# A gated linear-attention layer feeding a two-layer network on one core: first-chunk sums and state decays moved onto TensorE, one PSUM pool, and a new order of steps

## The chip, the core and the metric

The kernel runs on one core of a Trainium2 chip. Its time is the device time of one execution in microseconds (us). Five instruction streams work side by side: TensorE (PE, with its weight loads, PEld), VectorE (DVE), ScalarE (ACT), GpSimd (POOL) and SyncE (SP), which here issues every DMA. Each stream takes its instructions strictly in the order in which the program wrote them, and waits where an operand, a buffer or a PSUM bank is not ready.

## What is computed

For 4 batches and 8 heads (32 sequences of 768 steps, head size 40) the reference runs an mLSTM cell, and then a feed-forward network on all 3072 tokens (320 to 2048 to 320):

```python
for t in range(S):                                   # S = 768
    m_new  = np.maximum(f_gate[:, :, t] + m, i_gate[:, :, t])
    f_stab = np.exp(f_gate[:, :, t] + m - m_new)
    i_stab = np.exp(i_gate[:, :, t] - m_new);  m = m_new
    C = f_stab * C + i_stab * np.einsum('bhd,bhe->bhde', vt, kt)
    n = f_stab * n + i_stab * kt
    h_tilde = np.einsum('bhde,bhe->bhd', C, qt)
    denom = np.maximum(np.abs(np.einsum('bhd,bhd->bh', n, qt)[:, :, None]), 1.0)
    y[:, :, t] = sigmoid(o_gate[:, :, t]) * h_tilde / denom
h = y_as_tokens @ w_in                               # 3072 x 320 @ 320 x 2048
g = np.where(h >= 1, h, np.where(h <= -1, 0.0, (h + 1) ** 2 / 4))
out = g @ w_out                                      # 2048 x 320
```

## The kernel before

**Tiles.** The 768 steps are cut into 6 chunks of 128. A tile n is one chunk of one batch (chunk n // 4, batch n % 4; 24 tiles, eight heads each). A tile has these steps: `load_qk`, `load_v`, `load_A` (loads); `score` (16 products of keys and queries into two PSUM banks, then two VectorE products with the decay matrix A, one for each half of four heads); `main` (16 products of the masked scores with the gated values; from chunk 1 on also products with the carried state; then the denominator z, the gated output y, three transposes, a cast and two subtractions, which put the tile's y as a pair of words xh, xl into the network's input X[j]); `carry` (from chunk 0 on: six products keys by values, a mask, the decay of the old state by `dec`, an addition).

**Decay matrices.** In chunk 0 (tiles 0 to 3) the matrix is built on TensorE: `exponents` (steps E) writes a causal mask of -30000 into two PSUM banks, `add_sums` (A) adds the running gate sum of the column step by products with a one-hot matrix `pick`, and `decay` (x) takes eight exponentials of 128x128, each with the row step's sum `nA` as its bias. `first_sums` (p) makes that `nA` for chunk 0. In chunks 1 to 4 the sums go through a DRAM tensor `a_d` and come back broadcast (`load_A`), POOL masks them, ACT takes the exponentials. The gates of chunks 1 to 4 are worked out in one batch: `batch_maxima` (b), `batch_sums` (g1), `batch_tail` (tail.1), `batch_exps` (exps.1). `batch_exps` also makes the decay of the state for each sequence and chunk, writes it to DRAM (`dc_d`) in 40 copies and reads it back in 12 DMAs of 4-byte elements into `dec`, which lies by head dimension. `decays` does the same for one chunk.

**Network.** 512 tokens (four tiles) are a block j. For each of 16 slices fc of the 2048 columns `mm1` makes 8 products (the weights as pairs of words wh, wl), `relu` two ACT passes, `largest` (max) one VectorE pass, and `mm2` (out) adds into four PSUM banks that stay open for the whole block. Before block 0 the weights come as packed words: `load_w` (W.k) loads one of 16 pieces of 768 or 640 KB into one of three buffers `wraw`, and `convert` (w.k, seven steps for a piece of w_in, five for one of w_out) turns it into fp32 on ACT and VectorE. The fourth step is the last that reads the piece's buffer.

**Order.** The string STEPS lists, one after the other, every step of chunk 0, of chunk 1 and of block 0, with loads and conversions in between; each engine's queue is that list cut down to its own instructions. The mark `--` ends the front: the pool `gate` is closed and the network's buffers take its place. After STEPS the blocks 1 to 5 run in a loop with attention tiles 8 to 23 laid in by a plan. A step `w9`, `w2` or `w1` in the front asks for that many products of a zero matrix ahead of the next PSUM tile (`hot`); by STEPS there are 32 of them. PSUM is cut into three pools: two banks for attention (`psa`), two for mm1 (`psh`), four for mm2 (`pso`); only in the front does `psum_a` deal all eight out in turn.

Of the kernel before, what the change touches and what calls it, by code (L numbers as in the profile page):

```python
# [111 lines left out]
def mlstm_ffn_kernel(ctx, tc, qk, qn, vk, og, fi0, fi, fib, w_in, w_out, cst, out):  # L112
# [23 lines left out]
    ident = const.tile([P, P], F32, name="ident")  # L136
# [66 lines left out]
    def batch_maxima():  # L203
# [798 lines left out]
```

## Time and profile before

| | |
|---|---|
| median of 3 runs | 504.64 us (503.70 to 505.88) |
| the profiled execution | 506.14 us, of which 504.4 us from its first to its last instruction |
| PE busy | 488.2 us (97%) |
| DVE, ACT, POOL busy | 338.5, 303.0, 112.8 us |
| mean granted TensorE clock | 0.983 |

The profile gives each engine's busy time, the clock that TensorE was granted, and for an instruction the idle time of its engine before it and what ended that. A busy PE is a PE with a product in flight: at the lower clock the same product stays longer, so a busy PE may also be a slow one.

### The profile page before, as it was taken

How to read it: one execution, taken by the hardware profiler on the slowest of the kernel's cores; microseconds unless marked ns; L12 is line 12 of the kernel's file. 1: busy time of each engine (PE TensorE's matmuls, PEld its weight loads, DVE VectorE, ACT ScalarE, POOL GpSimd, SP SyncE). 2: the span in 40 equal slices, each digit the busy share in tenths (PEclk: the TensorE clock that was granted, in tenths of full speed). 3: DMA queues.
4: the chain of work that ended last, by engine and by line, in shares of the span. 5: the costliest groups of instructions: out<-in, count | busy, mean ns of one | idle time of the engine just before them, and what ended most of it. 6: DMA issues, size and time to landing. Idle time of an engine off the chain costs nothing.

```text
span 504.4 us, 8805 instructions
## 1 busy us (share of the span) xinstructions
PE 488.2 (97%) x3396; PEld 419.2 (83%) x3399; DVE 338.5 (67%) x621; ACT 303.0 (60%) x576; POOL 112.8 (22%) x120
## 2 busy tenths in 40 slices
PE   8799979999999999999999989999999999999996
PEld 4687757877788899888899878889888889989996
DVE  5689767978778986668875668757666745544332
ACT  6548958768587446596355596444587544365553
POOL 3020421150422423122422235312321200000000
PEclk9959997999999999999999999999999999999999
DMA  8975585550631132231322332222431000010001
GB/s 231 291 248 180 148 268 195 214 187 3 192 116 60 68 110 91 71 114 57 104 43 84 120 123 109 68 79 63 157 104 58 16 1 1 0 54 0 1 2 52
DMA packets 29646, 51.48 MB, mean 102 GB/s; under 512 B 10060, under 2 KB 19940, under 8 KB 29604
## 3 DMA queue, kind: packets, MB, share of 16 engines
q1 hardware_dynamic: 29604, 50.92, 31.6%
q8 instruction: 27, 0.44, 0.4%
q14 instruction: 15, 0.12, 0.1%
HBM read 46.80 MB, written 4.04 MB: 101 GB/s over the span
## 4 chain that ended last, share of the span: by engine, by line
PE 74%; ACT 4%; DVE 1%; issue 0%; ACTq 0%
PE pso L98 31%; PE psh L98 30%; PE psa L98 13%; ACT Abc L98 1%; ACT L98 1%; ACT r L98 1%; ACT sig L98 1%; DVE y L98 0%; ACT gh L98 0%; DVE gl L98 0%; DVE r L98 0%; DVE sz L98 0%; DVE z L98 0%; ACTq L997 0%; DVE v L98 0%
## 5 line engine op out<-in xcount | busy, mean ns | idle before, releaser
L98 ACT ACTIVATE r<-psh,half 128x512 f32<-128x512 f32 x96 | 65.7, 685 | 95.1 <-PE psh L98 94.9
L98 DVE SCALAR_TENSOR_TENSOR r<-psh,r 128x512 f32<-128x512 f32 x96 | 66.0, 688 | 62.8 <-ACT r L98 62.4
L98 PE MATMUL pso<-oh,gh 128*128 128x320 f32 x320 | 100.8, 317 | 1.8 <-ACT gh L98 1.6
L98 PE MATMUL psh<-xh,wh 128*128 128x512 f32 x288 | 101.5, 406 | 0.0
L98 PE MATMUL psh<-xh,wl 128*128 128x512 f32 x288 | 99.8, 398 | 0.4 <-DVE wl L98 0.4
L98 PE MATMUL pso<-ow,gh 128*128 128x320 f32 x320 | 99.4, 312 | 0.0
L98 PE MATMUL pso<-oh,gl 128*128 128x320 f32 x320 | 95.6, 312 | 0.0
L98 DVE TENSOR_TENSOR gl<-r,gh 128x512 fp32r<-128x512 f32 x80 | 63.1, 789 | 40.7 <-ACT gh L98 40.5
L98 ACT CAST gh<-r 128x512 fp32r<-128x512 f32 x80 | 49.4, 618 | 54.2 <-DVE r L98 53.6
L98 PEld LDWEIGHTS pso<-oh,gh 128*128 128x128 f32 x320 | 60.1, 188 | 6.9 <-ACT gh L98 1.8
L98 PEld LDWEIGHTS psh<-xh,wl 128*128 128x128 f32 x288 | 54.5, 190 | 13.2 <-DVE wl L98 0.8
L98 PEld LDWEIGHTS pso<-ow,gh 128*128 128x128 f32 x320 | 60.2, 188 | 3.0
L98 ACT ACTIVATE r<-r 128x512 f32<-128x512 f32 x96 | 60.7, 632 | 2.7
L98 PE MATMUL psh<-xl,wh 128*128 128x512 f32 x192 | 62.0, 401 | 0.0
L98 PEld LDWEIGHTS pso<-oh,gl 128*128 128x128 f32 x320 | 59.3, 188 | 0.3
L98 PEld LDWEIGHTS psh<-xh,wh 128*128 128x128 f32 x288 | 50.5, 190 | 6.5 <-DVE r L98 0.2
L98 ACT ACTIVATE Abc<-Abc,nA 128x128 f32<-128x128 f32 x160 | 50.2, 391 | 0.8 <-POOL Abc L98 0.7
L98 POOL TENSOR_TENSOR v<-vk,G 128x328 f32<-128x328 f32 x36 | 30.4, 851 | 63.5 <-issue 42.5
L98 PEld LDWEIGHTS psh<-xl,wh 128*128 128x128 f32 x192 | 36.2, 190 | 8.4
L98 POOL TENSOR_SCALAR_AFFINE_SELECT Abc<-Abc 128x1024 f32<-128x1024 f32 x20 | 24.5, 1226 | 80.2 <-DMA Abc<-a_d 60.9
L98 PE MATMUL pso<-ow,r 128*128 128x320 f32 x128 | 37.7, 440 | 0.0
L98 POOL TENSOR_TENSOR m<-m 128x1024 bf16<-128x1024 f32 x12 | 23.4, 1949 | 50.6 <-DVE m L98 50.6
(174 smaller groups left out, 674.8 us busy)
## 6 DMA issues: line engine op xcount, KB each, us to landing
Abc<-a_d SPq DMA_DIRECT2D x20, 512.0 KB
raw<-in_qk SPq DMA_DIRECT2D x48, 160.0 KB
vk<-in_vk SPq DMA_DIRECT2D x20, 324.0 KB
wraw<-in_w_in SPq DMA_DIRECT2D x8, 768.0 KB
wraw<-in_w_out SPq DMA_DIRECT2D x8, 640.0 KB
sig<-in_og SPq DMA_DIRECT2D x6, 640.0 KB
out<-r SPq DMA_DIRECT2D x24, 160.0 KB
qn<-in_qn SPq DMA_DIRECT2D x20, 180.0 KB
```

Of the source, the lines that this page charges most:

```text
L98: r = getattr(self.engine, name)(*args, **kwargs)
```

## The change

It does seven things. (1) `first_sums` and `nA` for chunk 0 go; `add_sums` ends in a product with `less` (minus `pick`) in each half, which subtracts the row's sum in PSUM, and `decay` takes one exponential of 128x512 for each half. (2) `dc_d`, `dc`, `decays` and the 15 reads into `dec` go; `batch_decays` (decs) takes one exponential of a 128x16 one-hot matrix with the decay as its bias, three small products and one copy; `heads` (one) builds the left factor once on POOL. (3) All eight PSUM banks are one pool `ps`. (4) The zero products are asked for by steps of their own, `hot.k`, ten in all. (5) `batch_maxima`, `batch_sums` and `batch_tail` are cut into 2, 3 and 4 steps that can be placed apart. (6) The constants `head_of` and `own` come with `ident`. (7) STEPS is a new list, from the first load to the end of block 0. The mm, relu, max, out, W, w and attention steps of tiles 4 to 9 in it are the same in number.

```diff
-    ps_a = ctx.enter_context(tc.tile_pool(name="ps_a", bufs=2, space=PSUM))
-    ps_h = ctx.enter_context(tc.tile_pool(name="ps_h", bufs=2, space=PSUM))
-    ps_o = ctx.enter_context(tc.tile_pool(name="ps_o", bufs=4, space=PSUM))
+    ps = ctx.enter_context(tc.tile_pool(name="ps", bufs=8, space=PSUM))
...
+    less = gate.tile([3 * NSEQ, NSEQ], BF16, name="less")
+    nc.vector.tensor_scalar(out=less, in0=pick, scalar1=-1.0, scalar2=None, op0=ALU.mult)
...
-        dx = mid.tile([P, D], F32, name="dx_b")
-        nc.scalar.activation(dx, mb["dc"].broadcast_to([P, D]), AF.Exp)
-        nc.sync.dma_start(dc_d[1:5].rearrange("c b (h d) -> (c b h) d", d=D), dx)
+    def heads():
+        T["one"] = mb["all"][:, 1, :DM]
+        nc.gpsimd.tensor_copy(T["one"].rearrange("p (h d) -> p h d", d=D), head_of.unsqueeze(2).broadcast_to([P, H, D]))
+
+    def batch_decays(n):
+        e = mb["all"][:, 1, DM:DM + B * B]
+        nc.scalar.activation(e, own, AF.Exp, bias=mb["dc"])
+        dp = psum_a()[:120, :3 * B * B]
         for g, h0 in enumerate(GROUPS):
-            for c in range(1, 5):
-                nc.sync.dma_start(dec[:, g, :, c], dc_d[c, :, h0 * D:(h0 + 3) * D].rearrange("b x -> x b"))
+            nc.tensor.matmul(dp[:, g * B * B:(g + 1) * B * B],
+                             T["one"][:, h0 * D:(h0 + 3) * D], e, start=True, stop=True)
+        yield
+        nc.scalar.copy(dec[:, :, :, 1:5], dp.rearrange("p (g b c) -> p g b c", g=3, b=B))
...
                 nc.tensor.matmul(ps[hh][:, h * L:(h + 1) * L], pick[:, k:k + 1].broadcast_to([3 * NSEQ, P]),
-                                 top(T["ac"]), start=False, stop=h == 3)
+                                 top(T["ac"]), start=False, stop=False)
+            k = b * H + 4 * hh
+            nc.tensor.matmul(ps[hh], top(T["ac"]), less[:, k:k + 4].unsqueeze(2).broadcast_to([3 * NSEQ, 4, L]),
+                             start=False, stop=True)
...
+        if c == 0:
+            nc.scalar.activation(A[:, 4 * hh:4 * hh + 4, :], T[n]["Ap"][hh].rearrange("p (h t) -> p h t", t=L), AF.Exp)
+            return
...
-        hp = ps_h.tile([P, 512], F32, name="psh")[:, :TT]
+        hp = psum_a()[:, :TT]
```

The head of STEPS, up to the first steps of block 0, before and after (numbers behind a dot are tiles, pieces or halves; `fi`, `fb`, `qk`, `vv`, `v`, `og`, `id`, `cs`, `W`, `A` are loads; `mask` is the old E, `add` the old A, `dec` the old x, `gex` the old h):

```diff
-    "Lg Li Lo Lq0 Lv0 Lq1 Lw0 Lf Lq2 Lv2 Lq3 Lw1 Lc o w9 E0 g0 p A0 k0 x00 w2 s0 W.6 x01 m00 w1 E1 v.6 A1 h0 v0 "
-    "x10 m01 W.2 w2 s1 x11 v1 m10 c w2 u0 v.0 m11 b w2 E2 w.1 A2 x20 w2 s2 y0 w.1 x21 v2 w.1 m20 m21 w2 u1 w.1 z0 "
-    "w2 E3 A3 x30 e v2.0 w2 s3 v3 w.1 y1 x31 t0 m30 m31 w2 u2 z1 y2 w2 v.1 u3 v.3 t1 z2 qk.4 v2.1 w.2 W.3 y3 w2 "
-    "v.2 t2 z3 qk.5 w.2 og.1 v2.3 w.2 W.4 t3 d g1 -- A.4 v2.2 carry.0 carry.3 A.5 mm.0 mm.1 w.2 relu.0 w.2 carry.3 "
+    "fi.0 sums.0 mask.3 W.0 w.0 mask.1 gtail.0 mask.0 vv.0 w.0 qk.0 fb.0 mask.2 w.0 add.0 bmax.0 dec.0.0 qk.1 "
+    "add.1 w.0 id.0 add.3 dec.1.1 qk.2 add.2 score.0 w.0 dec.0.1 dec.2.0 dec.2.1 vv.2 gex.0 bmax.0 score.0 v1.1 "
+    "one.0 hot.2 score.1 score.0 og.0 v1.0 dec.1.0 score.2 score.1 score.1 score.2 v1.3 main.0 v1.2 score.2 main.1 "
+    "qk.3 W.1 v.0 bsum.0 v.4 dec.3.0 v.1 bsum.0 main.2 bsum.0 v.5 sig.0 btail.0 main.0 btail.0 btail.0 main.1 "
+    "score.3 dec.3.1 w.1 btail.0 main.0 main.0 hot.4 main.0 W.2 main.2 main.1 v2.0 exps.0 score.3 w.0 main.1 cs.0 "
+    "score.3 main.0 main.2 main.3 main.1 v2.4 carry.0 main.2 hot.2 main.1 main.3 decs.0 main.2 w.1 w.1 carry.4 "
+    "hot.2 w.1 main.3 main.3 main.2 main.3 W.3 w.2 A.5 v2.1 v2.5 A.4 w.0 W.4 w.2 w.1 main.3 carry.0 prep.5 carry.1 "
+    "qk.4 carry.5 W.5 -- w.2 w.2 w.2 qk.5 carry.1 mm.0 mm.1 relu.0 W.6 w.2 main.4 relu.1 w.3 carry.4 W.7 w.2 w.3 "
+    "max.0 main.5 mm.3 relu.3 w.3 decs.0 prep.4 v.6 mm.2 max.1 w.3 A.6 max.3 relu.2 v.2 main.5 carry.4 w.4 main.4 "
+    "w.4 w.3 max.2 v1.4 out.0 carry.5 prep.5 carry.5 w.4 w.4 A.7 prep.4 v1.5 qk.6 w.5 out.1 ..."
```

## Rows read from the trace of the kernel before

**Rows 1.** The page: its first line, the busy line, and the granted TensorE clock in 40 equal slices of the span (9 is 90% or more).

```profile
span 504.4 us, 8805 instructions
...
PE 488.2 (97%) x3396; PEld 419.2 (83%) x3399; DVE 338.5 (67%) x621; ACT 303.0 (60%) x576; POOL 112.8 (22%) x120
...
PEclk9959997999999999999999999999999999999999
```

**Rows 2.** Busy time by stage: the stretch, its length, busy time of PE, PEld, DVE, ACT and POOL (with instructions), then granted clock, DMA share and GB/s.

```profile
12.30:26.70 14.40, 11.82 (x104) 9.03 (x104) 9.60 (x18) 8.14 (x22) 1.17 (x2) 1.00 0.95 287
26.70:38.26 11.56, 11.35 (x57) 9.96 (x57) 9.62 (x27) 3.72 (x9) 3.56 (x5) 0.56 0.75 249
38.26:72.88 34.62, 33.70 (x187) 25.64 (x185) 26.29 (x54) 26.29 (x47) 8.26 (x8) 1.00 0.63 179
72.88:75.84 2.96, 0.00 (x0) 0.03 (x1) 2.75 (x5) 2.93 (x7) 0.00 (x0) 0.83 1.02 408
75.84:82.50 6.66, 6.66 (x21) 5.44 (x22) 5.55 (x10) 5.48 (x9) 1.09 (x1) 0.56 0.83 276
...
104.00:400.00 296.00, 293.54 (x2219) 256.30 (x2219) 215.96 (x381) 181.35 (x351) 86.65 (x81) 1.00 0.29 93
```

**Rows 3.** The timeline of the front, the first uses of three loads: start, duration, engine, operation; in brackets the engine's idle time before it and what ended it.

```profile
2.83 0.48 DVE L98 TENSOR_TENSOR_SCAN m<-fi,m 96x128 f32<-96x128 f32 x1 [1.91 <-DMA fi<-in_fi]
...
13.70 0.89 ACT L98 ACTIVATE mg<-wraw 128x768 f32<-128x768 f32 x1 [0.47 <-DMA wraw<-in_w_in]
...
17.47 0.74 POOL L98 TENSOR_TENSOR ow<-ow,G 128x328 f32<-128x328 f32 x1 [4.73 <-DMA ow<-in_vk]
```

**Rows 4.** The timeline of PE: tile 0's 16 products in `main`, tile 2's transposes, two zero products, tile 3's 16 products, two carries' 12 products, the first mm1, and one carry's six products in block 0.

```profile
12.86 1.88 PE L98 MATMUL psh<-ow,Abc 128*128 128x41 f32 x16
...
29.40 0.88 PE L98 MATMUL pso<-ident,y 128*128 128x128 f32 x3
30.07 1.06 PE L98 MATMUL psa<-zeros 128*128 128x512 bf16 x2
30.92 3.48 PE L98 MATMUL psa<-ow,A 128*128 128x41 f32 x16
...
36.84 1.67 PE L98 MATMUL psa<-ow 128*120 128x123 f32 x12
38.26 0.70 PE L98 MATMUL psh<-xh,wh 128*128 128x512 f32 x2
...
57.69 0.87 PE L98 MATMUL psa<-v,vk 128*120 128x123 f32 x6 [0.20 <-issue]
```

**Rows 5.** VectorE: groups by shape from 0 to 38.3 us (busy us and mean ns, then idle before them), and its busy time in the two stretches that hold the batch sums and the batch tail.

```profile
L98 DVE TENSOR_TENSOR Abc<-pso,Abc 128x512 f32<-128x512 f32 x4 | 2.8, 692 | 3.6 <-ACT Abc L98 3.6
...
L98 DVE TENSOR_TENSOR_SCAN m_r<-fi_r,m_r 32x512 f32<-32x512 f32 x1 | 1.8, 1821 | 0.0
...
L98 DVE TENSOR_TENSOR y<-psa,sz 128x320 f32<-128x320 f32 x2 | 1.0, 491 | 0.1
L98 DVE SCALAR_TENSOR_TENSOR win<-mg,win 128x768 int32<-128x768 int32 x1 | 1.0, 958 | 0.1
L98 DVE TENSOR_TENSOR xl<-psa,xh 128x256 fp32r<-128x256 f32 x2 | 0.8, 414 | 0.0
...
L98 DVE RECIPROCAL z<-z 128x8 f32<-128x8 f32 x4 | 0.8, 203 | 0.1
...
39.20:41.00 1.80, 1.66 (x8) 1.00 0.00 0
43.60:45.70 2.10, 1.96 (x9) 1.00 0.81 321
```

**Rows 6.** SyncE's queue: when a DMA instruction started and how long it held the queue.

```profile
19.35 5.34 SPq L98 DMA_DIRECT2D m_b<-m_r  x4
...
51.01 0.33 SPq L98 DMA_DIRECT2D dc_d<-dx_b  x1
56.64 7.05 SPq L98 DMA_DIRECT2D dec<-dc_d  x12
...
64.81 0.35 SPq L98 DMA_DIRECT2D wraw<-in_w_out  x1
```

**Rows 7.** The timeline around PE's longest wait.

```profile
72.02 0.77 ACT L98 ACTIVATE mg<-wraw 128x640 f32<-128x640 f32 x1 [5.33 <-DMA wraw<-in_w_out]
...
72.83 0.49 DVE L98 TENSOR_SCALAR mg<-mg 128x640 f32<-128x640 f32 x1 [3.27 <-ACT mg L98]
...
75.06 0.68 DVE L98 TENSOR_TENSOR Abc<-psa,Abc 128x512 f32<-128x512 f32 x1
...
75.84 1.55 PE L98 MATMUL psa<-v,vk 128*120 128x123 f32 x6 [2.96 <-issue]
```

**Rows 8.** ACT's groups by shape from 38 to 104 us, columns as in Rows 5.

```profile
L98 ACT ACTIVATE Abc<-Abc,nA 128x128 f32<-128x128 f32 x43 | 13.5, 389 | 0.7 <-POOL Abc L98 0.7
L98 ACT ACTIVATE r<-psh,half 128x512 f32<-128x512 f32 x10 | 6.7, 674 | 3.6 <-PE psh L98 3.6
...
L98 ACT ACT_TABLE_LOAD x2 | 2.6, 1283 | 0.0
...
L98 ACT CAST xh<-psa 128x384 fp32r<-128x384 f32 x2 | 0.9, 462 | 0.0
...
L98 ACT ACTIVATE dx_b<-dc_b 128x40 f32<-128x40 f32 x1 | 0.2, 248 | 0.0
```

More of the change, by code (lines that the diff above doesn't have):

```diff
@@ L134, in mlstm_ffn_kernel @@
     nc.gpsimd.memset(zeros, 0.0)
-    ident = const.tile([P, P], F32, name="ident")
+    id_t = const.tile([P, P + H + B * B], F32, name="ident")
+    ident = id_t[:, :P]
+    head_of = id_t[:, P:P + H]
+    own = id_t[:, P + H:]
     cs_t = const.tile([120, 9 * D1], F32, name="cs")
@@ L157, in mlstm_ffn_kernel @@
     nA = const.tile([P, NC, NSEQ], F32, name="nA")
-    dc = const.tile([NSEQ, NC], F32, name="dc")
-    dc_d = dr.tile([NC, B, H * D], F32, name="dc_d")
     dec = const.tile([120, 3, B, NC], F32, name="dec")
@@ L450, in mlstm_ffn_kernel, with hot @@
     W_ORDER = [(kind, i) for i in range(NFC // 2) for kind in ("in", "out")]
-    front = True
     late = None
-    turn = 0
     def psum_a():
-        nonlocal turn
-        turn += 1
-        if front:
-            k = turn % 8
-            if k > 1:
-                return ps_h.tile([P, 512], F32, name="psh") if k < 4 else ps_o.tile([P, 512], F32, name="pso")
-        return ps_a.tile([P, 512], F32, name="psa")
+        return ps.tile([P, 512], F32, name="ps")
     mark = {}
-    heat = 0
-    def hot(out):
-        nonlocal heat
-        for _ in range(heat):
+    def hot(k):
+        out = psum_a()
+        for _ in range(k):
             nc.tensor.matmul(out, zeros[:, :P], zeros, start=True, stop=True)
-        heat = 0
     sig = {}
@@ L570, in decay @@
         A = T[n]["A"]
+        if c == 0:
+            nc.scalar.activation(A[:, 4 * hh:4 * hh + 4, :], T[n]["Ap"][hh].rearrange("p (h t) -> p h t", t=L), AF.Exp)
+            return
         for h in range(4 * hh, 4 * hh + 4):
             bias = nA[:, c, b * H + h:b * H + h + 1]
[L573 to L574 removed]
+            nc.scalar.activation(A[:, h, :], A[:, h, :], AF.Exp, bias=bias)
     def scale1(n):
@@ L721, in mlstm_ffn_kernel @@
                 plan.setdefault(i0 + i, []).append((n, kind, i, k))
-    order = {"score": score, "main": main, "prep": prep, "carry": carry_on}
+    order = {"score": score, "main": main, "prep": prep, "carry": carry_on,
+             "bmax": batch_maxima, "bsum": batch_sums, "btail": batch_tail, "decs": batch_decays}
     gens = {}
@@ L805, in mlstm_ffn_kernel, with weights @@
     block = {}
-    def tile0(what):
-        kind, n, *_ = what.split(".") + [0]
-        n = int(n)
+    convs = {}
+    def weights(k, i=1):
+        if k not in convs:
+            convs[k] = convert(*W_ORDER[k])
+        for _ in range(i):
+            next(convs[k], None)
+    InOrder.on = True
+    do = {
+        "fi": lambda n: first_gates(),
+        "id": lambda n: nc.sync.dma_start(id_t, cst[:, :P + H + B * B]),
+        "cs": lambda n: nc.sync.dma_start(cs_t, cst[0:120, P + H + B * B:]),
+        "fb": lambda n: load_batch(),
+        "og": load_og, "qk": load_qk, "v": load_v, "vv": load_v2, "A": load_A,
+        "W": lambda n: load_w(*W_ORDER[n]),
+        "w": weights, "sig": sigmoid, "mask": exponents, "add": add_sums, "dec": decay,
+        "sums": lambda n: run(gate_sums(n)),
+        "gtail": lambda n: run(gate_tail(n)), "gex": gate_exps,
+        "v1": scale1, "v2": scale2,
+        "exps": lambda n: batch_exps(),
+        "hot": hot,
+        "one": lambda n: heads(),
+    }
+    for what in STEPS.split():
+        if what == "--":
+            gates.close()
+            mo = ctx.enter_context(tc.tile_pool(name="mo", bufs=2))
+            continue
+        kind, *ns = what.split(".")
+        ns = [int(n) for n in ns]
+        n = ns[0]
         if kind == "mm":
@@ L816, in tile0 @@
         elif kind == "out":
+            if not ops:
+                ops[0] = [psum_a() for _ in range(NTC)]
             mm2(ops[0], n, *gs.pop(n))
-        elif kind == "w":
-            weights(n)
-        elif kind == "W":
-            load_w(*W_ORDER[n])
-        elif kind == "og":
-            load_og(n)
-        elif kind == "sig":
-            sigmoid(n)
-        elif kind == "v":
-            load_v(n)
-        elif kind == "qk":
-            load_qk(n)
-        elif kind == "A":
-            load_A(n)
-        elif kind == "v1":
-            scale1(n)
-        elif kind == "v2":
-            scale2(n)
-        elif kind == "tail":
-            batch_tail()
-        elif kind == "exps":
-            batch_exps()
+        elif kind in do:
+            do[kind](*ns)
@@ L921, in mlstm_ffn_kernel @@
         if x < NG:
-            if fc == 0:
-                ops[j] = [ps_o.tile([P, 512], F32, name="pso") for _ in range(NTC)]
             if j == 1 and fc % 2 == 0:
@@ L940, in mlstm_ffn_kernel @@
             j, fc = divmod(x - LAG, NFC)
+            if fc == 0:
+                ops[j] = [psum_a() for _ in range(NTC)]
             mm2(ops[j], fc, *gs.pop(x - LAG))
@@ L978, in _layout @@
     a["w_out"] = moe_w_out.view(np.int64).reshape(NFC // 2, 2, P, DM).transpose(0, 2, 1, 3).reshape(NFC // 2, P, 2 * DM)
-    c = a["cst"] = np.zeros((P, P + 9 * D1), np.float32)
+    o = P + H + B * B
+    c = a["cst"] = np.zeros((P, o + 9 * D1), np.float32)
     c[:, :P] = np.eye(P)
+    c[:, P:P + H] = np.tile(np.eye(H), (P // H, 1))
+    c[:, P + H:o] = -30000.0
+    for r in range(P):
+        c[r, P + H + r // H % B * B + r // NSEQ] = 0
     for j in range(3):
-        c[0:120, P:P + 9 * D1].reshape(3, D, 3, 3, D1)[j, :, :, j, :] = 1
+        c[0:120, o:].reshape(3, D, 3, 3, D1)[j, :, :, j, :] = 1
     return {n: np.ascontiguousarray(a[n]) for n in _INS}
```

106 lines of the change are left out of this document (13 added, 93 removed), and 29 rows, old and new, of the table STEPS.

## The prediction, made before the changed kernel was run

> **What bounds the kernel now.** I read the page first: PE is busy for 97% of the span, and its clock is low in two slices only, the third (25 to 38 us) and the seventh (76 to 88 us) [rows 1]; a clock of 0.5 in the rows is the lower of its two levels, 1.2 against 2.4 GHz. So the question is not which engine is full but when PE gets useful work, and at which clock. The stages answer that [rows 2]. From 104 to 400 us PE is busy 293.5 of 296 us at full clock; a new order in the front can't touch that. Block 0's first product starts at 38.26 us [rows 4]; what lies ahead of it is a chain, not PE work. After it come 34.6 us almost without a gap, then 2.96 us in which PE does nothing, then 6.66 us at a mean clock of 0.56 [rows 2]. The end therefore moves by three things: when block 0's first product starts, how much PE work is already done by then, and what becomes of that gap and its slow clock.
>
> The gap, read backwards [rows 7]: PE starts a carry at 75.84 when VectorE's masking of scores at 75.06 has emptied a bank of `psa`, the pool with two banks. VectorE was late by a conversion that waited 3.27 us for ACT, and ACT had waited 5.33 us for a piece of w_out. SP issued that piece at 64.81 only, because the decay's write at 51.01 and its 12 reads from 56.64, which held the queue 7.05 us, stood ahead of it [rows 6].
>
> **The front, after the change.** VectorE's list up to block 0 sets a floor. When does it start? `bmax` stands in VectorE's queue ahead of the first masking of scores and needs the gate rows fi_r. In the kernel before, the pieces queued ahead of and with W.0 (by their shapes 2,536 KB) had landed at 13.70, and those up to the second `vv` (3,440 KB) at 17.47 [rows 3]: 240 KB/us. (From the first load, 96 KB at 2.83, to W.0 it is 224.) The new list puts 768 KB of W.0 ahead of `vv.0` and `qk.0`: 1,640 KB up to fi_r, so 13.7 - 896 / 240 = 10.0 us. The scan takes 1.82 [rows 5]: VectorE is free for the rest at 11.8 us. Ahead of tile 3's decay-masked scores it then has: two conversion steps, under 0.96 each, 1.6; eight halves of scores at 0.69, 5.5; batch sums 1.66 and batch tail 1.96; three z at about 0.55 (three operations of 0.2 or less); two sz and two y at 0.49, 2.0 [rows 5]. That is 14.4, and 1.0 for some 35 starts at 0.02 to 0.04 apart (the two batch stretches show 0.28 us idle in 17 instructions): 27.2 us.
>
> From there PE's list rules, and its clock decides. Tile 3's 16 products take 1.88 us at full clock and 3.48 at half [rows 4]. Behind them PE has, in order: a carry, tile 2's transposes, two zeros, three small decay products, a carry, two zeros, tile 3's transposes. At half clock: 0.84 (half of the row of 12), 0.88, 1.06, 0.3, 0.84, 1.06, 0.88 [rows 4], 5.9 in all, so 27.2 + 3.5 + 5.9 = 36.6; then a cast 0.46 [rows 8] and two subtractions of 0.41 and less [rows 5]: 37.8. Two more carries hold PE to 38.3, and wl of W.0 (under 0.96) is there at 38.8. SP adds a risk: its four `m_b` DMAs held the queue 5.34 us [rows 6], and the new list has og.0, qk.3 and W.1 behind them; I allow 0.2 us. First product of block 0 at 39.0, **+0.7** against 38.26. At full clock the same list is bound by VectorE: 27.2, then 1.88 on PE beside 2.4 of other tiles' subtractions and outputs, z, two conversion steps, sz and y of tile 3 (0.6 + 1.0 + 1.0), transposes, cast and subtractions 1.6, wl 1.0, the same allowance and 0.5 for starts: 35.5, or -2.8.
>
> Which clock? Before, PE was at half from about 27 us on although the list put zeros ahead of almost every group, and a stretch with 11.82 of 14.40 us busy went ahead of it [rows 2]. The new list has 10 zeros where 32 were, and PE waits some 2 us for tile 0's y. I take half.
>
> The Trainium skill (TensorE: Matmul & The Clock Gate, Part 1: The HAM clock gate) says that the throttled clock is the default and that activity is what lifts it; by that rule fewer zeros make the front cold for longer, which is rival 2 below (501.0). The fall at 27 us in a busy but thin stretch agrees with it [rows 2].
>
> **Work that is done earlier.** Two carries more than before stand ahead of block 0 (0, 1, 4 and 5; before, a row of 12 products, two carries), and the four transposes of the batch. A carry takes up to 0.87 in block 0 at full clock [rows 4], less when the next group follows at once, so 0.7; four transposes 0.6 (three took 0.88 at half). 2 x 0.7 + 0.6 = **-2.0** behind block 0's start.
>
> **The gap and its clock.** The 13 decay DMAs go: SP is not held from 51.01 to 63.69, and the piece of w_out would come up to 12.7 us earlier, against a wait of 5.33. Beside that PE finds four free banks next to mm2's four, for whoever asks, where attention had two. So 2.96 goes, and of the 6.66 us behind it 6.66 x (1 - 0.56) = 2.93: **-5.89**. The bounds are 0 (the gap has another cause) and -5.89.
>
> **What I cost at nothing.** One exponential per half: 0.67 for 4 x 0.39 [rows 8], about 7 us less on ACT in the front; but ACT is busy 3.72 of 11.56 us where the front is decided [rows 2], so nothing comes of it, nor of one more pair of table loads (2 x 1.28 [rows 8]), since the sigmoid now stands between exponentials; without that slack it would cost 2.6. The exponential, products and copy of the decays: 0.25, 0.3, 0.25 on ACT and PE by the row of `dx_b` [rows 8], inside the list above; if they are late, `carry.4`'s decay on POOL waits, and that waited before. The eight `less` products, under 0.53 each at half clock like the zeros [rows 4], and four masks run while PE waits for keys and queries; uncovered they would cost 4. `one` on POOL, under 1 us, runs ahead of `v1.0` and is covered by VectorE's conversions. One PSUM pool from 104 us on: at most it gains the 2.46 us that PE idles up to 400 [rows 2]; at worst each of five changes of mm2's banks waits like the one bank wait I can see, 2.96 [rows 7], +14.8. PE is idle for only 0.8% of that stage, and the number of banks is the same, so I take 0; the range stops short of the far end.
>
> **Sum.** +0.7 - 2.0 - 5.89 = -7.2. Against the profiled span that is 504.4 - 7.2 = 497.2, and its own time 506.14 becomes 498.9. The profiled execution is slower than all three runs shown; their median is 504.64, so the median forecast is **497.4**. What a measurement of this kernel can tell from no change is 0.5%, 2.5 us: faster means under 502.1, slower over 507.2.
>
> **Rivals.**
> (1) *The front runs at full clock.* For it: the masks and scores at 15 to 22 us are now denser. Against: the wait for tile 0's y. Block 0 starts at 35.5, sum -2.8 - 2.0 - 5.89 = -10.7: 493.9.
> (2) *The clock falls already in `main` 0 to 2*, which now follow each other without zeros. Then `main` 2, the scores of tile 3 and two transposes take double, about 1.6 + 1.0 + 1.0 more ahead of tile 3's products: block 0 at 42.6, sum +4.3 - 2.0 - 5.89 = -3.6: 501.0. Before, clock 1.00 up to 26.7 speaks against it [rows 2].
> (3) *The gap stays or comes back elsewhere.* In it VectorE was busy 2.75 and ACT 2.93 of 2.96 us [rows 2]: both engines are full, and a DMA that comes earlier only lets them be late somewhere else. Then -2.0 + 0.7 = -1.3: 503.3, no change.
> (4) *Slower: SP stands at buffers.* `wraw` has three buffers. W.6 is issued ahead of w.3's fourth step and W.7 ahead of w.4's, and SP can't pass them; v.6, A.6, v.2, A.7 and qk.6 stand behind. Before, a hold of SP of 12.7 us ended in a gap of 2.96 us and 2.93 of slow clock. If the new hold makes PE idle for 8 us, its cost is 8 + 2.9, and the time 497.4 + 10.9 = 508.3. It decides from 6.9 us of idle on (497.4 + 9.8 = 507.2). Against it: v.2 is needed for a carry that is not on PE's path until tile 6's turn, and the DMA share is 0.63 in this stage [rows 2].
>
> **Chances.** Forecast 0.38, (1) 0.24, (2) 0.12, (3) 0.14, (4) 0.12. Under 502.1 lie the forecast, (1), and three quarters of (2) less what the forecast loses to small new waits: 0.68 faster; no change 0.19 ((3) and the rest); slower 0.13. The range reaches below (1) by the pool's 2.46 and half a microsecond of front, 491; above it takes in (3) and the lower part of (4), 507.
>
> **What would show it.** Right: block 0's first product near 39 us, half clock before it, no SP row between the batch exponentials and the next loads, no ACT wait of 5 us for a piece of w_out, no PE gap over 1 us between 40 and 130 us, clock 1.00 there. The front step is wrong if block 0 starts before 37 or after 41. The gap's step is wrong if a gap of 2 us or more, with a low clock behind it, stands anywhere in block 0. The whole is wrong if PE's idle time from 104 to 400 us moves by more than 2 us, which would be the pool or the loop's order.

## Result and the profile after

The changed kernel takes 487.83 us (median of 4 runs, 486.16 to 488.63) against 505.26 us for the kernel before on the same chip: a ratio of 0.9655, 95% interval [0.9618, 0.9692]. The prediction had the sign and less than half of the size (497.4, range 491 to 507). The profiled execution took 486.16 us, 484.4 of it from first to last instruction, 20.0 us less than before's 504.4. The medians and ranges of the experiments below leave out executions that took over 1.5% longer than the fastest of the same kernel (one in each of three experiments, two of ten in another, and two of four in `after_zeros_between`, which took 669.7 and 668.7 us at a mean granted clock of 0.65).

The page after the change, to be read beside [rows 1]: its first line, the busy line, the granted clock in 40 slices, and the DMA packets.

```profile
span 484.4 us, 8765 instructions
...
PE 475.2 (98%) x3390; PEld 412.3 (85%) x3390; DVE 330.7 (68%) x619; ACT 299.8 (62%) x553; POOL 115.4 (24%) x121
...
PEclk9689999999999999999999999999999999999999
...
DMA packets 22029, 51.44 MB, mean 106 GB/s; under 512 B 2443, under 2 KB 12323, under 8 KB 21987
```

The second low slice, at 76 to 88 us in [rows 1], is gone; what is left is one low stretch near the start. PE's busy time fell by 13.0 us with only six products less.

The stages after, columns as in [rows 2]: the low-clock stretch, the rest of the front, block 0 in two parts, and blocks 1 to 5.

```profile
16.60:26.80 10.20, 10.20 (x51) 8.82 (x51) 8.15 (x29) 4.30 (x5) 0.74 (x1) 0.50 1.02 323
26.80:33.84 7.04, 7.04 (x62) 6.40 (x61) 4.80 (x14) 3.93 (x9) 2.22 (x4) 1.00 0.97 328
33.84:75.00 41.16, 40.84 (x236) 32.35 (x235) 35.09 (x61) 33.98 (x61) 13.16 (x12) 1.00 0.68 224
75.00:116.80 41.80, 41.80 (x222) 32.81 (x221) 34.74 (x66) 34.84 (x65) 6.84 (x8) 1.00 0.61 193
116.80:474.60 357.80, 356.10 (x2671) 317.05 (x2670) 232.85 (x414) 211.75 (x399) 86.08 (x77) 1.00 0.22 68
```

Block 0 has 0.32 us of PE idle, and the loop runs at full clock. The same stage of the kernel before, slice 16 to slice 95:

```profile
130.95:494.70 363.75, 361.29 (x2671) 320.87 (x2670) 235.64 (x412) 212.65 (x399) 83.42 (x76) 1.00 0.21 70
```

The same 2671 products took 361.3 us of busy PE before and 356.1 after.

**Three stages as a yardstick.** ACT's first pass of relu starts when a slice's mm1 is done. Its starts for slice 0, 16 (block 1) and 95 (the last) cut any run of this kernel into a front, block 0, and a loop; what is behind slice 95 is 9.6 us before and 9.7 after. All values are us, from the profiled executions:

| kernel | slice 0 | 16 | 95 | block 0 | loop | median of runs |
|---|---|---|---|---|---|---|
| before | 41.2 | 131.0 | 494.7 | 89.8 | 363.8 | 505.26 |
| after | 36.3 | 116.8 | 474.6 | 80.5 | 357.8 | 487.83 |
| difference | -4.9 | | | -9.3 | -6.0 | -17.4 |

The three differences make -20.1, the -20.0 of the spans. By the medians it is 17.4, since before's profiled execution lies 0.9 above its median and after's 1.7 below.

### The profile page after: what moved, and what is told of

Its sections match the earlier page's. It is cut to its first block, busy times and chain, and to the rows that moved or that the text cites. A ratio compares the mean times of both kernels' runs of the same rounds, so it can differ in the third digit from the quotient of the medians.

```text
span 484.4 us, 8765 instructions
## 1 busy us (share of the span) xinstructions
PE 475.2 (98%) x3390; PEld 412.3 (85%) x3390; DVE 330.7 (68%) x619; ACT 299.8 (62%) x553; POOL 115.4 (24%) x121
## 4 chain that ended last, share of the span: by engine, by line
PE 89%; DMA 3%; DVE 3%; ACT 2%; issue 1%; POOL 1%; ACTq 0%; SPq 0%; DVEq 0%
PE ps L102 89%; DMA ident<-in_cst 1%; DMA out<-r 1%; DMA wraw<-in_w_in 1%; ACT r L102 1%; ACT L102 1%; POOL m L102 0%; POOL v L102 0%; DVE win L102 0%; DVE mg L102 0%; ACT sig L102 0%; DVE ow L102 0%; DVE xl L102 0%; DVE r L102 0%; DVE C L102 0%
## 5 line engine op out<-in xcount | busy, mean ns | idle before, releaser
L102 ACT ACTIVATE r<-ps,half 128x512 f32<-128x512 f32 x96 | 66.0, 687 | 103.0 <-PE ps L102 102.0
L102 DVE SCALAR_TENSOR_TENSOR r<-ps,r 128x512 f32<-128x512 f32 x96 | 66.1, 688 | 60.0 <-ACT r L102 59.5
L102 PE MATMUL ps<-oh,gh 128*128 128x320 f32 x320 | 102.3, 320 | 0.0
L102 PE MATMUL ps<-xh,wh 128*128 128x512 f32 x288 | 101.1, 405 | 0.1
L102 PE MATMUL ps<-ow,gh 128*128 128x320 f32 x320 | 99.4, 311 | 0.0
L102 PE MATMUL ps<-xh,wl 128*128 128x512 f32 x288 | 98.1, 395 | 0.0
L102 PE MATMUL ps<-oh,gl 128*128 128x320 f32 x320 | 97.6, 310 | 0.0
L102 PEld LDWEIGHTS ps<-oh,gh 128*128 128x128 f32 x320 | 60.2, 188 | 3.0
L102 PEld LDWEIGHTS ps<-ow,gh 128*128 128x128 f32 x320 | 60.3, 188 | 1.7
L102 PE MATMUL ps<-xl,wh 128*128 128x512 f32 x192 | 60.6, 396 | 0.0
L102 POOL TENSOR_TENSOR v<-vk,G 128x328 f32<-128x328 f32 x36 | 30.7, 852 | 98.3 <-issue 44.1
L102 POOL TENSOR_SCALAR_AFFINE_SELECT Abc<-Abc 128x1024 f32<-128x1024 f32 x20 | 25.0, 1257 | 53.0 <-DVE v L102 14.2
```

Of the source, the lines that this page charges most:

```text
L102: r = getattr(self.engine, name)(*args, **kwargs)
```

## Experiments

The theory from the two traces: the loop's 6 us are the shared PSUM pool, block 0's 9.3 us the decays that no longer hold SP, the front's 4.9 us the clock. The rival: the new order of steps carries most of it, and pool and decays are small. Every kernel below was run beside the kernel before, whose median was 502.4 to 505.7 us. The stages of all but `after_zeros_between`, whose profile can't be used:

| kernel | slice 0 | block 0 | loop | median (lowest to highest) | ratio to before |
|---|---|---|---|---|---|
| before_one_pool | 44.1 | 85.7 | 359.5 | 499.09 (495.79 to 500.71) | 0.9887 [0.9824, 0.9950] |
| before_onehot | 41.1 | 90.5 | 365.7 | 508.80 (507.53 to 511.74) | 1.0087 [1.0054, 1.0120] |
| after_banks_apart | 38.9 | 79.9 | 366.0 | 496.62 (493.63 to 500.23) | 0.9850 [0.9767, 0.9934] |
| after_dram_decays | 41.5 | 89.2 | 357.7 | 499.64 (495.04 to 502.44) | 0.9893 [0.9804, 0.9982] |
| after_old_order | 40.1 | 92.3 | 357.1 | 501.03 (498.41 to 503.79) | 0.9945 [0.9913, 0.9976] |
| old_order_decs_late | 39.5 | 88.6 | 358.9 | 497.93 (494.77 to 501.76) | 0.9873 [0.9813, 0.9934] |
| after_no_zeros | 40.5 | 79.9 | 358.0 | 489.59 (487.87 to 493.93) | 0.9734 [0.9653, 0.9815] |
| after_four_exps | 36.8 | 79.9 | 357.8 | 487.20 (485.94 to 487.39) | 0.9664 [0.9604, 0.9724] |
| after_ident_early | 38.5 | 79.9 | 358.4 | 487.55 (487.38 to 488.29) | 0.9681 [0.9631, 0.9730] |
| after_zeros_between_2 | 34.3 | 80.6 | 359.1 | 487.38 (485.53 to 490.18) | 0.9686 [0.9608, 0.9764] |
| after_zeros_early | 39.5 | 79.9 | 359.5 | 491.98 (487.81 to 494.77) | 0.9773 [0.9679, 0.9867] |

Two things can be read at once. The loop is 357 to 359.5 us in every kernel with one pool and 363.8 to 366.0 in the three with banks set apart, whatever the order of the front. Block 0 is near 80 only where the new order and the one-hot decays come together, always with one pool in block 0. The front spreads over 34.3 to 40.5 in kernels that hardly differ: `after_banks_apart` is the changed kernel's program up to block 1, and its slice 0 comes 2.6 us later (38.9 against 36.3), while its block 0 differs by 0.6. So a front that is read from one execution, the changed kernel's own 4.9 us too, is uncertain by some 2.6 us.

### One pool, put in and taken out

In the kernel before, the pool alone:

```diff
-    ps_a = ...tile_pool(name="ps_a", bufs=2, space=PSUM)    # and ps_h 2, ps_o 4
+    ps = ...tile_pool(name="ps", bufs=8, space=PSUM)
```

> The kernel before with one PSUM pool of eight banks (part 3 alone), same order, zeros and decays. Theory (the loop behind block 0 got 5 to 6 us shorter because attention and mm1 share four spare banks): the stretch from block 1's first relu (130.95 us before) to the end shrinks from 373.5 to about 368, and PE's gap of 2.96 us at 72.88 goes or shrinks, since the carry there no longer waits for a bank; time 495 to 499. Rival (the banks do nothing; the loop's gain comes with the order in which block 0 hands over): time 503 to 506 and 373 us from block 1 to the end.

In the changed kernel, from block 1 on, two fixed banks for mm1, two for attention, four for mm2:

```diff
+    fixed.update({k: [ps.tile([P, 512], F32, name="ps") for _ in range(2)] for k in ("h", "a")})
...
-        hp = psum_a()[:, :TT]
+        hp = psum_a("h")[:, :TT]
```

> The changed kernel, but from block 1 on mm1 has two banks of its own and attention two, used in turn, as in the kernel before; block 0 unchanged. Theory (the shared spare banks make the loop shorter): block 1's first relu at 117 as in the changed kernel, then 372 to 374 to the end instead of 367.6, time 492 to 494. Rival (loop gain is not the banks'): 487 to 489.

The pool took 4.3 us from the loop of the kernel before (363.8 to 359.5, in an execution that also lost clock for 3.4 us at 305), and setting banks apart gave 8.2 us back to the loop of the changed one. That is more than the theory said, and 496.62 us lies above its 492 to 494, since the front came 2.6 us later as well.

The pool alone also took PE's gap out of block 0 (89.8 to 85.7 us), with the decay DMAs still in place. SP and ACT, and then the stage that answers to the gap [rows 2, rows 7]:

```profile
58.82 6.79 SPq L98 DMA_DIRECT2D dec<-dc_d  x12
...
66.72 0.35 SPq L98 DMA_DIRECT2D wraw<-in_w_out  x1
...
73.06 0.79 ACT L98 ACTIVATE mg<-wraw 128x640 f32<-128x640 f32 x1 [2.38 <-DMA wraw<-in_w_out]
```

```profile
72.00:80.00 8.00, 7.97 (x41) 6.13 (x40) 6.96 (x11) 6.87 (x12) 1.09 (x1) 1.00 1.01 329
```

The reads hold SP for 6.79 us as before, the piece of w_out is issued no earlier (66.72 against 64.81) and ACT waits 2.38 us for it, yet PE is busy for 7.97 of 8.00 us at full clock. So by this run the chain through SP ended in a gap only while attention had two banks. (In this execution block 0 also began 2.9 us later, behind a front with 20.5 us of low clock, and PE waited 2.00 us for ACT up to 53.6.)

Where the loop's microseconds go shows in the group of the score products (`raw`: keys and queries, 15 tiles of 16) over the loop; columns: busy us, mean ns of one, idle before. Before, before with one pool, after, and after with the banks apart:

```profile
L98 PE MATMUL psa<-raw 40*128 40x128 f32 x240 | 23.6, 290 | 0.2 <-issue 0.2
```

```profile
L98 PE MATMUL ps<-raw 40*128 40x128 f32 x240 | 19.5, 288 | 0.0
```

```profile
L102 PE MATMUL ps<-raw 40*128 40x128 f32 x240 | 19.3, 286 | 0.0
```

```profile
L102 PE MATMUL ps<-raw 40*128 40x128 f32 x240 | 24.6, 291 | 0.3 <-DVE hv L102 0.3
```

With the same count and nearly the same mean, the group fills 4 to 5 us more wherever attention has two banks. The timeline of PE says why. Before, one tile's scores (a line for each run of equal products; nine products of the network lie in the omitted lines):

```profile
141.01 0.48 PE L98 MATMUL psa<-raw 40*128 40x128 f32 x2
141.42 0.41 PE L98 MATMUL pso<-oh,gh 128*128 128x320 f32 x1
...
143.33 0.40 PE L98 MATMUL psh<-xl,wh 128*128 128x512 f32 x1
143.66 1.16 PE L98 MATMUL psa<-raw 40*128 40x128 f32 x14
144.75 0.41 PE L98 MATMUL pso<-oh,gh 128*128 128x320 f32 x1
```

And after:

```profile
126.50 0.48 PE L102 MATMUL ps<-xh,wl 128*128 128x512 f32 x1
126.90 1.16 PE L102 MATMUL ps<-raw 40*128 40x128 f32 x16
```

The run of two takes 0.41 us up to the start of the next kind, and the run of fourteen then takes as long as a whole one of sixteen (143.66 to 144.75, 1.09 us, and 1.09 in the changed kernel as well): 0.41 us for a broken tile. The scores are broken off after two products in 13 of 15 tiles of the loop before (in 12 by other products, in one by a wait of 0.20 us) and in all 15 with the banks apart, but in 4 of 15 in the changed kernel and in 4 in the kernel before with one pool: nine or eleven tiles, 3.7 or 4.5 us. The same 4 of 15 tiles are broken in all ten kernels with one pool, and also in the execution at a mean clock of 0.65, so it is the list that differs and not the execution. Behind STEPS the program no longer fixes what may stand between two products; that the builder sets other work in where a bank is not free by its reckoning is the likely reason, but it was not shown. So some 4 of the 6 us are these broken runs (the group's 23.6 against 19.3); PE counts as busy through all of it, and no idle time shows it. The rest is spread over the other groups and wasn't traced.

### The one-hot decays, put in and taken out

In the kernel before, `batch_exps` ends in the exponential, three products and a copy instead of the 13 DMAs (and `decays`, whose values no state uses, goes):

```diff
-        nc.sync.dma_start(dc_d[1:5].rearrange(...), dx)      # and 12 reads into dec
+            nc.tensor.matmul(dp[:, g * B * B:(g + 1) * B * B], T["one"][:, h0 * D:(h0 + 3) * D], e, ...)
```

> The kernel before with the state decays by one-hot products in place of the DRAM round trip (part 2 alone). Theory (SP's queue held by the decay DMAs made PE's gap and the slow clock behind it): no gap at 72.88, no stretch of clock 0.5 near 75 to 82, time 498 to 500. Rival (the gap is a bank's or VectorE's): gap of 2 to 3 us stays, time 503 to 505.

It came out 3.1 us slower than the kernel before, outside both ranges. In the profiled executions it is 2.6 us, of which 0.7 are block 0, and 1.9 the loop, where the clock was low for 3.4 us from 301.8. ACT, POOL and PE around the new wait in block 0:

```profile
48.44 1.28 ACT L98 ACT_TABLE_LOAD   x1
...
49.62 1.09 POOL L98 TENSOR_SCALAR_AFFINE_SELECT Abc<-Abc 128x1024 f32<-128x1024 f32 x1 [12.28 <-DVE C L98]
...
50.43 0.32 ACT L98 ACTIVATE fi_r<-ident,dc_b 128x16 f32<-128x16 f32 x1
50.65 0.45 POOL L98 COPY fi_r<-ident 128x320 f32<-128x320 f32 x1
...
51.16 1.38 PE L98 MATMUL psa<-fi_r 128*120 128x16 f32 x6 [4.19 <-POOL fi_r L98]
```

The gap at 75 us is gone, as the prediction's chain through SP says. (The pool alone took it away too.) But in the old order the three small products stand on PE's list straight behind the batch transposes, while their left factor waits on POOL behind a masking that had waited 12.28 us, and their exponential on ACT behind the sigmoid and two table loads. PE stands still for 4.19 us with all of block 0 queued behind, and during this wait, at 49.3, the clock falls for 6.8 us.

The other way, the changed kernel with the DMAs put back at the places of the two `decs` steps:

```diff
-        nc.scalar.copy(dec[:, :, :, 1:5], dp.rearrange("p (g b c) -> p g b c", g=3, b=B))
+        for g, h0 in enumerate(GROUPS):
+            for c in range(1, 5):
+                nc.sync.dma_start(dec[:, g, :, c], dc_d[c, :, h0 * D:(h0 + 3) * D].rearrange("b x -> x b"))
```

> The changed kernel with the decays written to DRAM in 40 copies and read back in 12 DMAs again, at the place of the decay steps. Theory (those DMAs hold SP's queue for some 12 us and what stands behind them is late): PE gaps of 2 us or more in block 0 with a slow clock behind, time 491 to 495. Rival (the new order has the loads far enough ahead, the DMAs cost nothing): 487 to 489.

Block 0 goes from 80.5 to 89.2 and the loop stays; with a later front on top, the time lies above the theory's range. SP, POOL, VectorE and PE:

```profile
22.66 0.35 SPq L102 DMA_DIRECT2D cs<-in_cst  x1
34.45 0.33 SPq L102 DMA_DIRECT2D dc_d<-dx_b  x1
...
54.51 7.06 SPq L102 DMA_DIRECT2D dec<-dc_d  x12
...
63.30 0.80 POOL L102 TENSOR_TENSOR C<-C,dec 120x369 f32<-120x369 f32 x1
...
64.14 0.55 DVE L102 TENSOR_TENSOR C<-C 120x369 f32<-120x369 f32 x1 [9.04 <-POOL C L102]
...
66.23 1.19 PE L102 MATMUL ps<-xh,wh 128*128 128x512 f32 x2 [5.25 <-DVE Abc L102]
```

SP issues nothing from 23.01 until its write at 34.45, which waits for ACT's exponential, and the reads hold it 7.06 us, as in [rows 6]. But it is not the old gap that comes back: here it is VectorE's addition of a state that stands 9.04 us for the decay, and PE 5.25 us for a masking queued behind that, with the clock low for 6.8 us from 64.3. The front is also 5.2 us later, of which a part is the clock (low for 20.5 us from 13.1, after PE had waited 1.48 us for the identity's DMA, 0.44 in the changed kernel); no run tells how much of the rest is SP's standing still in the front.

### The old order with the new code

> The changed kernel's code (one pool, one-hot decays, first chunks' differences on TensorE, one exponential a half) with the kernel before's written-out order of steps and its 32 zeros. Theory: the order carries about half of the gain, the front's 4.4 us and the place of the decay products. The pool's loop time stays (loop from first relu of slice 16 to that of 95 about 358), the decay products again stand right behind the sigmoid and the two table loads, so block 0 stays near 90 as in the run with the one-hot decays alone: 497 to 501 us. Rival, that the code's parts alone carry the gain and the order is free: 488 to 491 us, block 0 near 81.

The edit is STEPS alone: the list of the kernel before, in the names of the changed one, with its 32 zeros. The time is the upper end of the theory's range: beside the kernel before on the same chip (503.7) the code without its order is worth 2.7 us of the 17.4. The loop is 357.1, so the pool's share stays. PE waits where it did in the run with the one-hot decays:

```profile
50.89 1.39 PE L102 MATMUL ps<-fi_r 128*120 128x16 f32 x6 [4.73 <-POOL fi_r L102]
```

Against the changed kernel's block 0 (11.8 us less) the groups of PE in the two show 6.0 us less idle time, 2.9 us less in the network's products for the clock's 6.8 low us, 2.8 us of work that the new order has done before block 0 (12 of 24 products of states, 1.8, four batch transposes, 1.0), and the one-hot products, 1.4, done there as well. (The groups overlap a little, so the parts make more than 11.8.) The front, which takes that work on, is still 3.8 us shorter.

So the loop's share is the pool's, as the theory has it, and in block 0 and the front little is gained without the new order, as the rival has it; but block 0 needs the one-hot decays too (89.2 with the DMAs). The parts don't add up singly: one pool alone is worth 6.6 us by the medians, the one-hot decays alone cost 3.1, and each costs some 8 to 12 us when it is taken out of the changed kernel. The new order on the old code was not run.

Then the two `decs.0` alone were moved in the old order, behind the products of slices 2 and 3:

```diff
-    ... sig.1 exps.0 one.0 decs.0 decs.0 prep.5 w.4 v1.4 mm.2 max.1 w.3 v2.4 mm.3 score.4 ...
+    ... sig.1 exps.0 one.0 prep.5 w.4 v1.4 mm.2 max.1 w.3 v2.4 mm.3 decs.0 decs.0 score.4 ...
```

> As the run with the changed code in the old order, but the six one-hot products of the decays and the copy of their result are moved behind the first layer's products of slices 2 and 3, some 14 us of TensorE's work later. Theory: in the old order the decay products stand at the head of TensorE's queue 4.7 us before their exponential and the GpSimd copy are done, and the clock then falls for 6.8 us; moved, that wait goes (4.7 us) and with it the slow stretch (3.4 us), block 0 falls from 92.4 to 84 to 87 us and the time from 501.0 to 493 to 496.5 us. Rival: the wait is one of a chain (the loads, W.5, the scores behind), so that it comes up at the next product: 498 us or more.

The time, 497.93, is the rival's 498 or just below it. Block 0 fell from 92.3 to 88.6, not to 84 to 87, because the wait came up once more at the next product:

```profile
49.29 0.73 PE L102 MATMUL ps<-xh,wh 128*128 128x512 f32 x2 [1.77 <-ACT nA L102]
```

The mm1 product needs a bank that the batch transposes fill and ACT empties, behind the same sigmoid and table loads. The low stretch shrank from 6.8 to 3.4 us. By the ratios to the kernel before (0.9945 and 0.9873) the move is worth some 3.6 us, and their intervals overlap.

### Exponentials, and the front's clock

Four exponentials of 128 columns in each half of the first chunks:

```diff
-            nc.scalar.activation(A[:, 4 * hh:4 * hh + 4, :], T[n]["Ap"][hh]..., AF.Exp)
+            for h in range(4):
+                nc.scalar.activation(A[:, 4 * hh + h, :], T[n]["Ap"][hh][:, h * L:(h + 1) * L], AF.Exp)
```

> The changed kernel with four exponentials of 128 columns in place of one of 512 in each half of a first chunk (8 halves, 1.56 us by the 389 ns row of the trace instead of 0.60). Theory: ScalarE has room between 11 and 25 us and the front is set by VectorE's masks and TensorE's products, so the time stays within 1.5 us of the changed kernel: 487 to 489.5 us. Rival: ScalarE then feeds TensorE's products of tiles 0 to 3 too late, 8 times 0.96 us of it: block 0's first product 3 to 7 us later and 491 to 495 us.

All stages within 0.6 us of the changed kernel: one exponential a half is worth nothing here. Four take 0.79 to 0.83 us against 0.60 for one, not the 1.56 expected.

The changed kernel without its ten zeros (`hot.k` taken out of STEPS):

> The changed kernel without its ten products of zeros. Theory: the zeros at 24.5 us are what keeps TensorE at work ahead of tile 3, so that the granted clock is back at 26.8; without them the low stretch that begins at 16.6 lasts longer than 10.2 us, tile 3's sixteen products take about 3.5 us instead of 1.88, block 0's first product goes from 33.8 to 36 to 39 and the time is 490 to 493 us. Rival: the clock comes back of itself 10.2 us after it fell, and the zeros only cost their about 2.9 us of TensorE, most of it in time TensorE would spend waiting: 486 to 488.5 us.

Its clock:

```profile
13.10:30.20 17.10, 17.05 (x93) 16.26 (x92) 11.31 (x35) 6.27 (x9) 3.40 (x6) 0.50 0.96 292
```

The low stretch is 17.1 us and block 0's first product comes at 36.52, as the theory had it (tile 3's products, at 30.19, just missed it). But the median lies between the two ranges, its interval overlaps the changed kernel's, and the identity landed late in this execution (PE waited 1.10 us for it). The run with the decay DMAs, where PE waited 1.48 us for it, has all ten zeros, and its clock fell at the same 13.1 us and stayed low for longer, 20.5 us. So the longer stretch can't be put down to the missing zeros. The identity's DMA was then moved to the head of the queue:

```diff
-    "fi.0 sums.0 mask.3 W.0 ... add.1 w.0 id.0 add.3 ...
+    "fi.0 id.0 sums.0 mask.3 W.0 ... add.1 w.0 add.3 ...
```

> The changed kernel with the identity's transfer put right behind the gate logits' at the head of the queue, so that the first transpose does not wait for it (0.44 us at 11.2, followed by the products of 41 columns during which the clock falls at 16.6). Theory: block 0's first product moves by under 1 us either way, since the front is a chain through VectorE's masks and conversions: 486 to 489 us. Rival: the wait is what lowers the clock; without it TensorE stays at the full clock from 16.6 to 26.8, the 48 products of tiles 0 to 2 take about 5.6 us instead of 8.0 and block 0 begins 2 to 4 us earlier: 483.5 to 486 us. Other rival: the logits and raw tiles behind it land later and the front is 0.5 to 1 us longer.

The wait for the identity goes and one of 0.56 us for keys and queries comes at 14.2; the clock falls at 18.2 for 10.2 us all the same. Block 0's first product comes at 35.19, 1.35 us later and not within 1 us, and the time is that of the changed kernel. Then seven more zeros were set among the steps that issue the narrow products (41 columns) of tiles 0 to 2:

```diff
-    ... score.2 v1.3 main.0 v1.2 score.2 main.1 qk.3 ...
+    ... score.2 v1.3 main.0 hot.1 v1.2 score.2 main.1 hot.1 qk.3 ...
```

> The changed kernel with seven more products of zeros, one behind each of seven of the steps that issue the 48 products of 41 columns of tiles 0 to 2. Theory: the clock falls at 16.6 us because of what TensorE does between 9 and 16 us (small loads and products of few columns, and the 0.44 us wait), so zeros between the narrow products bring it back earlier or keep it: the low stretch is 0 to 7 us, and block 0's first product comes 1 to 3 us earlier than 33.84: 485 to 487 us. Rival: VectorE's masks and conversions set the front, the first product stays within 0.5 us: 487 to 488.5 us. Other rival: the zeros come too late to change the clock and cost their 7 times 0.3 to 0.6 us: 488.5 to 491 us.

The two times, 485.95 and 491.69 us, tell nothing apart, and no stages can be read from this run. The same kernel once more:

> The kernel with seven more products of zeros between the narrow products of tiles 0 to 2 once more, since the profiled execution of the first time ran at a granted clock of 0.65 throughout and its stages can't be read; its two other executions gave 485.95 and 491.69 us, with mean clocks of 0.995 and 0.984. Theory: the zeros keep the clock up for most of the stretch from 16.6 to 26.8, the 48 products take 5.6 to 6.5 us instead of 8.0, but the front is by now as much VectorE's as TensorE's (VectorE idles only 3.5 us between 20.9 and 29), so block 0's first product comes 0 to 2.5 us earlier and the time is 485 to 488 us. Rival: the clock falls as before, the zeros cost 2 to 4 us: 489 to 492 us.

Stages of this run, and PE's timeline:

```profile
16.60:26.80 10.20, 9.97 (x87) 8.52 (x86) 8.77 (x31) 6.11 (x10) 1.70 (x3) 1.00 1.02 322
...
287.00:295.00 8.00, 7.20 (x78) 5.91 (x79) 7.00 (x15) 4.56 (x12) 3.62 (x4) 0.79 0.27 87
```

```profile
11.90 0.30 PE L102 MATMUL ps<-ident,ex 128*128 128x128 f32 x1 [1.20 <-DMA ident<-in_cst]
...
16.76 0.39 PE L102 MATMUL ps<-zeros 128*128 128x512 bf16 x1
...
18.69 0.39 PE L102 MATMUL ps<-zeros 128*128 128x512 bf16 x1
...
25.25 1.88 PE L102 MATMUL ps<-ow,A 128*128 128x41 f32 x16
...
31.84 0.71 PE L102 MATMUL ps<-xh,wh 128*128 128x512 f32 x2
...
287.80 0.20 PE L102 MATMUL ps<-v,m 128*128 128x41 bf16 x1 [1.59 <-POOL m L102]
```

Here the clock stays up through the whole front although the identity came as late (1.20 us) as without zeros. That the added zeros hold it isn't shown. Only two of the seven run between narrow products, one behind each of the first two tiles' sixteen, and the first starts at 16.76, when the changed kernel's clock had already fallen (16.56): up to there the two kernels run the same products. Four other executions of this kernel had mean clocks of 0.984 to 0.995, by which (an estimate, twice the missing share of the span) 5 to 16 us of each ran at half clock.

Block 0 begins 2.0 us earlier than in the changed kernel (31.84 against 33.84). Of that the loop gives 1.3 back: behind PE's wait of 1.59 us for POOL the clock fell at 289.6 for 3.4 us, which it did not do in the changed kernel's execution behind the same wait. The median, 487.38, is in the theory's range, but it can't be told from the changed kernel's 487.83.

Last, the same seven zeros without the eight later ones:

> The same seven products of zeros between the narrow products of tiles 0 to 2, without the eight later ones (at 24.5, 30.0 and 31.7 us in the changed kernel, 3.1 us of TensorE). Theory: with the clock up early the later zeros hold nothing, and TensorE's 3.1 us before block 0 come free, of which VectorE's conversions let 1 to 2 us through: first product at 31 to 33 us, 484 to 487 us. Rival: without them the clock falls once more between 24 and 34 us, in the stretch of transposes and state products, and block 0 starts at half clock: 488 to 493 us.

```profile
20.07 1.27 ACT L102 ACTIVATE sig<-sig 128x1280 f32<-128x1280 f32 x1 [5.38 <-DMA sig<-in_og]
21.36 1.28 ACT L102 ACT_TABLE_LOAD   x1
22.65 0.60 ACT L102 ACTIVATE A<-ps 128x512 f32<-128x512 f32 x1
```

```profile
23.30 1.01 PE L102 MATMUL ps<-zeros 128*128 128x512 bf16 x2 [2.75 <-ACT A L102]
```

The time is in the rival's range. The clock was low from 20.6 to 30.9 us:

```profile
20.60:30.90 10.30, 7.60 (x38) 5.81 (x37) 5.26 (x13) 5.42 (x10) 2.11 (x3) 0.50 1.04 322
```

Up to 20.6 this kernel runs the same products as the one above, where the clock stayed up, so the missing zeros didn't lower it. PE's wait of 2.75 us had just begun then (20.55), and it has another reason: the output gate's logits let the sigmoid start at 20.07 (17.79 in the run above, 18.49 in the changed kernel), and behind it on ACT stand a table load and tile 3's second exponential, whose PSUM bank PE waits for until 23.30. Whether the missing zeros have a part in the rest can't be told from this run. No kernel of the study beats the changed one by more than the runs scatter.

## Why the prediction was wrong

**The front: +0.7 forecast, -4.4 measured** (first mm1 product, 38.26 to 33.84). The timeline of PE that answers to [rows 4]:

```profile
13.84 8.02 PE L102 MATMUL ps<-ow,Abc 128*128 128x41 f32 x48
21.78 2.08 PE L102 MATMUL ps<-raw 40*128 40x128 f32 x16
...
24.49 1.91 PE L102 MATMUL ps<-zeros 128*128 128x512 bf16 x4
...
27.26 1.88 PE L102 MATMUL ps<-ow,A 128*128 128x41 f32 x16
...
33.84 0.71 PE L102 MATMUL ps<-xh,wh 128*128 128x512 f32 x2
```

Tile 3's sixteen products were to begin at 27.2 and began at 27.26, but not for the reason given. VectorE's list was two microseconds ahead of its sum (the gate rows had landed by 9.00, not 10.0, the scan took 1.27, not 1.82, and tile 3's scores were masked by 25.2), while PE was two late, since the clock had fallen at 16.6, in the products of tiles 0 to 2. The step that failed is "I take half": from tile 3 to the first mm1 product 11.8 us were forecast and 6.58 passed, because the clock was back at 26.8. By the prediction's own two sums (39.0 and 35.5) the clock is worth 3.5 of these 5.2 us; the other 1.7 weren't traced. It was no single accident: in the four executions with this front that did not wait over 0.6 us for a load (the changed kernel, banks apart, four exponentials, identity early) the low stretch was 10.2 us and ended at 26.8 to 28.5. What ended it stays open. The forecast read the clock of the old order's late front into the new one. Rival (2) had the fall right, in `main` 0 to 2, and its consequence wrong; rival (1) had the late front's clock right. The Trainium skill (TensorE: Matmul & The Clock Gate, Part 1: The HAM clock gate), by which activity lifts the clock, was taken as speaking for fewer zeros being colder. The runs don't settle it: with no zeros the low stretch was 17.1 us, with ten 10.2 in four executions and 20.5 in one, with seventeen none in the one that was profiled. In the changed kernel PE was busy for 10.20 of 10.20 us at 0.50, so a PE that is busy in the profile was not enough to lift it there; nor did the fall at 27 us behind 11.82 busy us of 14.40 [rows 2] speak for that reading, as the prediction says.

**Block 0: -7.9 forecast, -9.3 measured.** The number held. The gap [rows 7] and its slow clock went (-2.96 and -2.93 forecast). The prediction gave two reasons for it at once, SP's freed queue and the free banks, and by the runs either one alone removes the gap at 75 us. With the decay DMAs put back into the changed kernel another gap opens (5.25 us), by another chain: POOL's decay of a state waits for the reads. Rival (3) is false for the change as a whole and true for the one-hot decays alone, where 4.19 us of PE idle took the gap's place. What the prediction lacked is that its covers, "if they are late, `carry.4`'s decay on POOL waits", named the wrong party: in the old order it is PE's own list that stands behind the three products. The work done earlier was -2.0 and is 2.8 by the rows of the old-order run, 4.2 with the one-hot products.

**The pool: 0 forecast, -6.0 measured.** This is the term that was mis-sized: its best case was bounded by PE's idle time, 2.46 us from 104 to 400 [rows 2]. The gain did not come out of idle time. PE idles 1.7 us in the loop now, against 2.5, and is busy for 5.2 us less, 4.3 of it in the group with the broken runs of scores. Nor did the sign that the prediction set for this term show: PE's idle time from 104 to 400 us moved from 2.46 to 1.70, by less than 2.

**The rest.** One exponential a half at nothing: right, by the run with four, though its 7 us less on ACT were too many, since four exponentials took 1.14 to 1.16 us in the kernel before's front and not 4 x 0.39. Rival (4), SP at its buffers: block 0 has no wait above 0.31 us, so it did not come. The four `m_b` DMAs held SP 2.48 us instead of 5.34 [rows 6]. The sum with the three measured stages, -4.9 - 9.3 - 6.0, against -7.2: 5.6 of the missing 13 us are the front, 6.0 the pool, 1.4 block 0.

## What to carry to other kernels

A bound taken from an engine's idle time holds only if its list stays as it is; when buffers are pooled and a builder orders the list, count how often runs of equal products are broken, and price a break from the starts (0.41 us a tile here). A small operation that replaces a DMA moves the wait to the engine whose list it enters: place it there behind work that covers its inputs, or the replacement gains nothing (508.80 us against 505.72 with the DMAs). A clock read from one order says little about another; give it a rival on each side with its full price, and read it from more than one execution before you name a cause. When two parts of a change can each remove a wait, put each in alone: the gap in block 0 went with either.

## What the runs showed of the hardware that was not expected

The granted clock stood at 0.50 for 10.2 us (16.6 to 26.8) with PE busy for 10.20 of them, at first in products of 41 columns. Of two kernels that run the same products up to 20.6 us, the clock fell at 20.6 in the one's execution and stayed at 1.00 in the other's, so what a list of products does to the clock can't be read from one execution. A PE wait of 1.4 to 1.6 us for POOL or ACT near 288 to 305 us was followed by 3.4 us of low clock in five of the profiled executions and by none in seven others; among the kernels with one pool the loops of the former are 358.9 to 359.5 us, of the latter 357.1 to 358.4.
